# An mLSTM mixer kernel: moving one weight residual behind xd, summing blocks 2 and 3 first, and doubling x's last columns on ScalarE in the last batch

## The chip, the cores and the metric

The kernel runs on one core of a Trainium2 chip. The metric is the device time of one execution in microseconds (us), as the median over several runs. The engines are named as in the profile: PE is TensorE (PEld its weight loads), DVE is VectorE, ACT is ScalarE, POOL is GpSimd, and SP issues the DMAs.

## The reference

Two parts follow each other. An mLSTM attention runs over 4 batches, 8 heads, 768 steps and head size 40; its output is x, 768 x 320 in each batch. Then a mixer works on x:

```
h  = np.maximum(x.T @ w_tok1, 0) @ w_tok2      # over tokens, 768 -> 256 -> 768
u  = x + h.T
h2 = np.maximum(u @ w_ch1, 0) @ w_ch2          # over channels, 320 -> 1536 -> 320
out = u + h2
```

## The kernel before

The recurrence is computed in chunks of 128 steps, so each batch has six blocks of 128 tokens, numbered s = 0 to 5. Matrix products keep float32 accuracy by splitting each operand into a high part and a low residual (names that end in h and l) and summing three products. The attention of batch b+1 is issued in small steps between the mixer's matmuls of batch b.

In the mixer of one batch, `a_part` (L698) and `a_end` (L706) make the first token product. `phase_b` (L734) then makes the second token product of block s in a PSUM bank ps_b. It adds the product to x on VectorE (`add_x`, L737) and calls `split_x` (L741), which makes xd: the last 64 columns of x twice side by side. In batches 1 to 3 xd is one VectorE copy (L745). In batch 0 its first half is a ScalarE copy (L747), and its second half is a subtraction on GpSimd (L748). `phase_t` (L751) transposes block s on PE with three matmuls (L760 to L762, the third one reads xd). ScalarE copies the high part into uT (L763), and VectorE writes the low parts (L764, and L766 in batches 1 to 3).

The channel products follow in slots. Batches 0 and 3 are "wide": in each of the first 12 slots, `gemm1w` (L793) multiplies one 128-column piece of c1 by blocks 0 to 3 at once (512 columns, L800). `gemm2w` (L807) adds the results of the slot before into four accumulators: blocks 0 and 1 in the banks ps_acc (k = 0), blocks 2 and 3 in ps_m (k = 1). When the last piece (i = 11) is in, `end` (L820) adds each sum to x on VectorE (L823) and sends the block out. Blocks 4 and 5 go through narrower slots after that (`gemm1`, L772, and `gemm2`, L826).

Every engine takes its instructions in the order in which the Python code emits them. In the last batch this order is written out by hand: the full `phase_b` of blocks 0 and 1, and then

```
for s in range(4):
    phase_t(b, s, ss)
    phase_b(b, s + 2)
```

In batch 0 the order around the change is: blocks 0 and 1 through `phase_b`, `dec_hi` (ScalarE rounds two weight pieces to their high parts, L682), `dec_low` (GpSimd makes both low residuals, L688), blocks 2 and 3 through `phase_b`, then the transposes. `dec_low` takes all the residuals that wait in the list `lows`.

In batch 0, slot 12 is the first slot after the wide ones. It runs `gemm1` of block pair 2, then both halves of `gemm2w` for i = 11, and then six steps of the next batch's attention, which take the next ps_m bank for the output po (L432, L438).

Of the kernel before, what the change touches and what calls it, by code (L numbers as in the profile page):

```python
# [12 lines left out]
AF = mybir.ActivationFunctionType  # L13
# [4 lines left out]
B, H, S, D = 4, 8, 768, 40  # L18
# [16 lines left out]
def kernel(ctx: ExitStack, tc: tile.TileContext, gates, qk, q3, kv, og,  # L35
                            wt1, wt2, wc1, wc2, ident, out):
    nc = tc.nc
# [9 lines left out]
    def f32(x):  # L47
        return x.bitcast(F32)
# [578 lines left out]
    his, lows, wx, early = [], [], [], [True]  # L627
# [54 lines left out]
            nc.scalar.activation(d[0][:, a:a + WP], f, AF.Copy)  # L682
            lows.append((f, d, a))

    def dec_low():
        while lows:
            f, d, a = lows.pop(0)
            nc.gpsimd.tensor_tensor(d[1][:, a:a + WP], f, f32(d[0][:, a:a + WP]), ALU.subtract)  # L688


    def mm3(ps, pairs, first, last):
        n = len(pairs)
        for i, (a, m) in enumerate(pairs):
            nc.tensor.matmul(ps, a, m, start=(first and i == 0), stop=(last and i == n - 1))  # L694
# [39 lines left out]
    def phase_b(b, s, pool=(ps_m, "m"), add=True):  # L734
        return [*halves_b(b, s, pool, add)][-1]
# [5 lines left out]
    def split_x(b, s):  # L741
        x = xs[(b, s)][0]
        xd = lp.tile([128, 2, 64], F32R, tag="xd", name="xd", bufs=3)
        if b:
            nc.vector.tensor_copy(f32(xd), x[:, 256:320].unsqueeze(1).to_broadcast([128, 2, 64]))  # L745
        else:
            nc.scalar.activation(xd[:, 0], x[:, 256:320], AF.Copy)  # L747
            nc.gpsimd.tensor_tensor(xd[:, 1], x[:, 256:320], f32(xd[:, 0]), ALU.subtract)  # L748
        XD[(b, s)] = f32(xd)

    def phase_t(b, s, pool=(ps_m, "m")):  # L751
        x = xs[(b, s)][0]
        k = s // 2
        xd = XD.pop((b, s))
        if s == 0:
            UP[b] = lp.tile([128, 2, 5, 256], F32R, tag="uT", name="uT", bufs=1)
        u = U[(b, k)] = UP[b][:, k % 2]
        a = slice((s % 2) * 128, (s % 2) * 128 + 128)
        ps = pool[0].tile([128, 3, 128], F32, tag=pool[1], name="ps_t")
        nc.tensor.transpose(ps[:, 0, :], x[:, 0:128], id_t)  # L760
        nc.tensor.transpose(ps[:, 1, :], x[:, 128:256], id_t)
        nc.tensor.transpose(ps[:, 2, :], xd.rearrange("p a c -> p (a c)"), id_t)  # L762
        nc.scalar.activation(u[:, 0:3, a], ps, AF.Copy)  # L763
        nc.vector.tensor_tensor(u[:, 3:5, a], ps[:, 0:2, :], f32(u[:, 0:2, a]), ALU.subtract)  # L764
        if b:
            nc.vector.tensor_tensor(u[64:128, 2, a], ps[64:128, 2, :], f32(u[64:128, 2, a]), ALU.subtract)  # L766
# [23 lines left out]
    def wide(b):  # L790
        return b in (0, B - 1)
# [15 lines left out]
    def gemm2w(b, i, gh, gl, half=None):  # L807
        if i == 0 and half != 1:
            for k, (pool, tag) in enumerate(((ps_acc, "acc"), (ps_m, "m"))):
                acc[k] = [pool.tile([128, DM], F32, tag=tag, name=f"acc{j}") for j in range(2)]  # L810
        a = slice(i * DM, (i + 1) * DM)
        tiles = [(k, tt, slice(tt * 128, (tt + 1) * 128)) for k in range(2) if half in (None, k) for tt in range(2)]
        for k, tt, t in tiles:
            mm3(acc[k][tt], [(gh[:, k, t], c2[x][:, a]) for x in range(2)], i == 0, False)
        for k, tt, t in tiles:
            mm3(acc[k][tt], [(gl[:, k, t], c2[0][:, a])], False, i == NF - 1)
            if i == NF - 1:
                end(b, k, tt)

    def end(b, k, tt):  # L820
        s = 2 * k + tt
        x = xs[(b, s)][0]
        nc.vector.tensor_tensor(x, acc[k][tt], x, ALU.add)  # L823
        nc.sync.dma_start(out=out[b, s * 128:(s + 1) * 128, :], in_=x)
# [15 lines left out]
    def step(g, n=1):  # L840
        for _ in range(n):
            next(g, None)
# [150 lines left out]
    for b in range(B):  # L993
        if b:
            for j in range(2):
                for s in range(NC - 1):
                    a_part(b, j, s)
        if b == 1:
            step(ag)
        if b:  # L1000
            gemm2(*pend, half=0)
        for j in range(2):
            a_part(b, j, NC - 1)
            a_end(b, j)
        if b:
            gemm2(*pend, half=1)
            pend = None
            first = [halves_b(b, s) for s in range(2)]
            for g in first * 2 if b < B - 1 else first:
                step(g, 1 if b < B - 1 else 2)  # L1010
            if b < B - 1:
                phase_b(b, 2, ss)
                phase_t(b, 0)
                phase_t(b, 1)
                step(ag, 2)
                phase_b(b, 3, ss)
            else:
# [3 lines that stand above are left out]
                step(ag)  # L1021
        slots = [(k, p) for k in range(3) for p in range(6)]
        if b == 0:
            pf = prep_first(units[NC], units[NC + 1])
            cols()
            sp.release()
            wx += [tc.alloc_tile_pool(name="wx", bufs=1, side="right"), nxt[0]]
            ep.release()
            pp.release()
            lp = ctx.enter_context(tc.tile_pool(name="lp", bufs=2))  # L1030
            step(dg, 9)
            dec_load(nxt[2] + 7)
            dg = dec_ops(9)
            phase_b(b, 0)
            phase_b(b, 1)
            dec_hi()
            dec_low()
            step(dg, 1)
            phase_b(b, 2, ss)
            step(dg, 1)  # L1040
            phase_b(b, 3, ss)
            phase_t(b, 0)
            phase_t(b, 1)
            add_x(b, 4, phase_b(b, 4, ss, add=False))
            phase_t(b, 2)
            phase_t(b, 3)
            t5 = phase_b(b, 5, ss, add=False)
            step(dg, 9)
            add_x(b, 5, t5)
            dec_hi()  # L1050
        more = {1: [(phase_b, 4, ss)], 2: [(phase_t, 2, ss), (phase_t, 3, ss)], 5: [(phase_b, 5, ss)],
                6: [(phase_t, 4), (phase_t, 5, ss)]}
        for n, (k, p) in enumerate(slots):
            if b == 0 and 2 < n < 11:
                step(dec_ops(9), 9)
            if wide(b) and n < NF:
                g = gemm1w(b, n, 1 if n < 1 else 0 if b else 2)
            else:
                g = gemm1(b, k, p, 1 if n == 0 else 0)
            if b == 0:  # L1060
                if n < 3:
                    dec_hi()
                    dec_abs(nxt[2] + 2, both=True)
                    dec_low()
                    step(dec_ops(9, order=((0, 0), (0, 1), (1, 0), (1, 1))), 9)
                if n == 2:
                    for _ in range(2):
                        dec_hi(1)
                        dec_abs(nxt[1] + 1)
                    dec_low()  # L1070
                if n == 10:
                    split_x(0, 4)
                    split_x(0, 5)
                if n == 11:
                    phase_t(0, 4, ss)
                    phase_t(0, 5, ss)
                    gemm2(*pend)
                    pend = None
                    wx[0].release()
                    wq.release()  # L1080
                    xpool[1] = ctx.enter_context(tc.tile_pool(name="xp", bufs=1, side="right"))
                    step(ag)
                if n < 11:
                    if n > 2:
                        dec_abs(nxt[2] + 2)
                        dec_hi()
                        dec_low()
                    if n in (8, 9):
                        sigmoid(1, (n - 8,))
                    if n > 5:  # L1090
                        step(pf)
                elif n > 11:
                    o = STEPS0[n - 12]
                    step(ag, o[0])
                    gemm2(*pend, half=0)
                    step(ag, o[1])
                    gemm2(*pend, half=1)
                    pend = None
                    step(ag, o[2])
            else:  # L1100
                for f, *a in more.get(n, ()) if not wide(b) else ((phase_t, 4, ss), (phase_t, 5, ss)) if n == 11 else ():
                    f(b, *a)
                step(ag, STEPS[n])
            if pend:
                gemm2(*pend)
            pend = (b, k, n if wide(b) and n < NF else p) + g
# [53 lines left out]
```

## Time and profile before

| | |
|---|---|
| median of 3 runs | 428.86 us (428.62 to 430.13) |
| the profiled execution | 428.82 us, of which the traced span is 426.9 us |
| granted TensorE clock over the span | 1.00 |
| busy: PE, PEld, DVE, ACT, POOL | 98%, 93%, 68%, 43%, 34% |

The busy share of PE comes from modelled ends of pipelined matmuls, so the distance between two starts tells more than the end of one. The times below are microseconds from the start of the span.

### The profile page before, as it was taken

How to read it: one execution, taken by the hardware profiler on the slowest of the kernel's cores; microseconds unless marked ns; L12 is line 12 of the kernel's file. 1: busy time of each engine (PE TensorE's matmuls, PEld its weight loads, DVE VectorE, ACT ScalarE, POOL GpSimd, SP SyncE). 2: the span in 40 equal slices, each digit the busy share in tenths (PEclk: the TensorE clock that was granted, in tenths of full speed). 3: DMA queues.
4: the chain of work that ended last, by engine and by line, in shares of the span. 5: the costliest groups of instructions: out<-in, count | busy, mean ns of one | idle time of the engine just before them, and what ended most of it. 6: DMA issues, size and time to landing. Idle time of an engine off the chain costs nothing.

```text
span 426.9 us, 9017 instructions
## 1 busy us (share of the span) xinstructions
PE 419.8 (98%) x3509; PEld 396.5 (93%) x3510; DVE 291.4 (68%) x650; ACT 185.1 (43%) x426; POOL 143.1 (34%) x186
## 2 busy tenths in 40 slices
PE   8999999999999999999999999999999999999996
PEld 4888988988999999999999999999999998888996
DVE  8989778735676688788796698789786647111412
ACT  5977567893544635234224246334144112111111
POOL 7587476852453411341341230331350110000000
PEclk9999999999999999999999999999999999999999
DMA  7997747860968612334455031432320000000000
GB/s 215 274 280 251 247 128 247 279 195 29 264 191 239 220 54 66 115 117 110 148 160 187 28 107 33 145 114 90 124 85 32 0 20 15 0 2 0 30 33 31
DMA packets 24574, 52.34 MB, mean 123 GB/s; under 512 B 2565, under 2 KB 13325, under 8 KB 24533
## 3 DMA queue, kind: packets, MB, share of 16 engines
q1 hardware_dynamic: 24293, 51.61, 39.7%
q8 instruction: 27, 0.44, 0.4%
q10 hardware_dynamic: 240, 0.18, 0.2%
q14 instruction: 14, 0.11, 0.1%
HBM read 47.73 MB, written 4.04 MB: 121 GB/s over the span
## 4 chain that ended last, share of the span: by engine, by line
PE 90%; DMA 4%; DVE 2%; POOL 2%; ACT 1%; issue 1%; SPq 0%; POOLq 0%; ACTq 0%
PE acc L694 30%; PE ps_h L781 21%; PE ps_h L800 10%; PE ps_a L694 5%; PE ps_sc L312 5%; PE ps_b L694 4%; PE po L438 4%; PE po L408 3%; PE pu L385 2%; DMA wst<-in_wt_dram 2%; PE po L414 2%; DMA kvt<-in_kv_dram 1%; PE po L377 1%; PE ps_t L760 1%; PE ps_t L762 1%
## 5 line engine op out<-in xcount | busy, mean ns | idle before, releaser
L781 PE MATMUL ps_h<-uT,c1h 128*128 128x256 f32 x480 | 93.4, 282 | 0.0
L694 PE MATMUL acc<-c2h,gh 128*128 128x320 f32 x288 | 89.3, 319 | 0.0
L786 ACT ACTIVATE gh<-ps_h 128x512 fp32r<-128x512 f32 x48 | 28.6, 596 | 135.5 <-PE ps_h L781 135.5
L694 PE MATMUL acc<-c2l,gh 128*128 128x320 f32 x288 | 86.4, 309 | 0.0
L781 PEld LDWEIGHTS ps_h<-uT,c1h 128*128 128x128 f32 x480 | 76.9, 188 | 0.5
L781 PE MATMUL ps_h<-uT,c1l 128*128 128x256 f32 x288 | 74.3, 280 | 0.0
L787 DVE SCALAR_TENSOR_TENSOR gl<-ps_h,gh 128x512 fp32r<-128x512 f32 x48 | 33.0, 688 | 43.8 <-ACT gh L786 43.8
L694 PE MATMUL acc<-c2h,gl 128*128 128x320 f32 x288 | 61.9, 309 | 0.0
L694 PEld LDWEIGHTS acc<-c2h,gh 128*128 128x128 f32 x288 | 54.1, 188 | 1.6
L694 PEld LDWEIGHTS acc<-c2l,gh 128*128 128x128 f32 x288 | 54.2, 188 | 0.9
L781 PEld LDWEIGHTS ps_h<-uT,c1l 128*128 128x128 f32 x288 | 54.3, 188 | 0.0
L457 POOL TENSOR_TENSOR sig<-sig,ht 128x320 f32<-128x320 f32 x18 | 14.8, 820 | 99.4 <-DVE ht L418 91.2
L293 ACT ACTIVATE dd<-dd,bcol 128x128 f32<-128x128 f32 x144 | 45.8, 392 | 4.6 <-POOL dd L283 4.5
L694 PEld LDWEIGHTS acc<-c2h,gl 128*128 128x128 f32 x288 | 47.2, 188 | 0.1
L804 DVE SCALAR_TENSOR_TENSOR gl<-ps_h,gh 128x512 fp32r<-128x512 f32 x24 | 16.5, 689 | 41.1 <-ACT gh L803 41.1
L800 PE MATMUL ps_h<-uT,c1h 128*128 128x512 f32 x120 | 36.0, 394 | 0.0
L508 POOL TENSOR_TENSOR xl<-x,xh 128x320 fp32r<-128x320 f32 x18 | 15.8, 875 | 51.1 <-DVE xh L506 49.7
L322 DVE TENSOR_TENSOR dd<-ps_sc,dd 128x512 f32<-128x512 f32 x48 | 30.9, 681 | 2.6 <-PE ps_sc L312 2.6
L803 ACT ACTIVATE gh<-ps_h 128x512 fp32r<-128x512 f32 x24 | 14.2, 592 | 36.3 <-PE ps_h L800 36.3
L312 PE MATMUL ps_sc<-raw 64*128 64x128 f32 (+1 forms) x384 | 27.0, 282 | 0.0
L312 PEld LDWEIGHTS ps_sc<-raw 64*128 64x128 f32 (+1 forms) x384 | 23.2, 187 | 3.6 <-issue 1.8
L800 PEld LDWEIGHTS ps_h<-uT,c1h 128*128 128x128 f32 x120 | 22.1, 188 | 3.9
(153 smaller groups left out, 870.3 us busy)
## 6 DMA issues: line engine op xcount, KB each, us to landing
dd<-phi_d SPq DMA_DIRECT2D x18, 512.0 KB
wst<-in_wc_dram SPq DMA_DIRECT2D x22, 384.0 KB
kvt<-in_kv_dram SPq DMA_DIRECT2D x24, 324.0 KB
raw<-in_qk_dram SPq DMA_DIRECT2D x48, 160.0 KB
sig<-in_og_dram SPq DMA_DIRECT2D x8, 480.0 KB
out_dram<-x SPq DMA_DIRECT2D x24, 160.0 KB
q3t<-in_q_dram SPq DMA_DIRECT2D x20, 180.0 KB
wst<-in_wt_dram SPq DMA_DIRECT2D x8, 384.0 KB
```

Of the source, the lines that this page charges most:

```text
L293: nc.scalar.activation(dd[:, h, :], dd[:, h, :], AF.Exp, bias=bcol[:, c, HP * b + h:HP * b + h + 1])
L312: nc.tensor.matmul(t["s"][hf][:, h, :], r[:, 1, h, :], r[:, 0, h, :], start=True, stop=True)
L322: nc.vector.tensor_tensor(dd, t["s"][hf], dd, ALU.mult)
L438: nc.tensor.matmul(o, t["dd"][:, ROW[h], :], x, start=c == 0 and h == 0, stop=h == H - 1)
L457: nc.gpsimd.tensor_tensor(sg, sg, ht[:, :, 0:D], ALU.mult)
L508: nc.gpsimd.tensor_tensor(xl, x, f32(xh), ALU.subtract)
L694: nc.tensor.matmul(ps, a, m, start=(first and i == 0), stop=(last and i == n - 1))
L781: nc.tensor.matmul(ps[:, j, :], c1[x][:, a:a + 128], u[:, y, :], start=part is first and i == 0 and (order == 0 or j == 0), stop=i == len( ...
L786: nc.scalar.activation(gh, ps, AF.Relu)
L787: nc.vector.scalar_tensor_tensor(gl, ps, 0.0, f32(gh), op0=ALU.max, op1=ALU.subtract)
L800: nc.tensor.matmul(ps, c1[x][:, a:a + 128], u[:, :, y, :], start=n == 0, stop=n == len(todo) - 1)
L804: nc.vector.scalar_tensor_tensor(gl, ps, 0.0, f32(gh), op0=ALU.max, op1=ALU.subtract)
```

## The change

In batch 0 one of the two waiting residuals stays where it was, and the other goes behind the xd of blocks 2 and 3 on GpSimd. The other calls of `dec_low` take up to four, which is all that waits there. In the wide slots, blocks 2 and 3 are summed ahead of blocks 0 and 1; where the sum is split in halves, the first half is now blocks 2 and 3. In the last batch xd is made by one ScalarE instruction of 128 columns.

```diff
-    def dec_low():
-        while lows:
+    def dec_low(n=4):
+        for _ in range(min(n, len(lows))):
...
         if b:
-            nc.vector.tensor_copy(f32(xd), x[:, 256:320].unsqueeze(1).to_broadcast([128, 2, 64]))
+            last2 = x[:, 256:320].unsqueeze(1).to_broadcast([128, 2, 64])
+            if b < B - 1:
+                nc.vector.tensor_copy(f32(xd), last2)
+            else:
+                nc.scalar.activation(f32(xd), last2, AF.Copy)
...
-        tiles = [(k, tt, slice(tt * 128, (tt + 1) * 128)) for k in range(2) if half in (None, k) for tt in range(2)]
+        tiles = [(k, tt, slice(tt * 128, (tt + 1) * 128)) for k in (1, 0) if half in (None, 1 - k) for tt in range(2)]
...
             phase_b(b, 0)
             phase_b(b, 1)
             dec_hi()
-            dec_low()
+            dec_low(1)
             step(dg, 1)
             phase_b(b, 2, ss)
             step(dg, 1)
             phase_b(b, 3, ss)
+            dec_low()
             phase_t(b, 0)
```

## Rows read from the trace of the kernel before

**Rows 1.** The page, chain that ended last: share of the span by engine.
```profile
PE 90%; DMA 4%; DVE 2%; POOL 2%; ACT 1%; issue 1%; SPq 0%; POOLq 0%; ACTq 0%
```

**Rows 2.** Busy time by stretch: each engine, granted clock, DMA share, GB/s.
```profile
343.00:362.00 19.00, 18.98 (x123) 17.91 (x122) 11.15 (x30) 4.03 (x8) 1.51 (x2) 1.00 0.05 19
362.00:398.00 36.00, 36.00 (x203) 32.36 (x201) 6.89 (x10) 5.83 (x10) 0.00 (x0) 1.00 0.00 0
```

**Rows 3.** Waits of PE's weight loads: who waited for whom, total, times, longest.
```profile
PEld po L438 <- DVE x L823: 0.4, 1, 0.4
```

**Rows 4.** Timeline of POOL, batch 0: start, us, engine line operation.
```profile
53.53 1.98 POOL L688 TENSOR_TENSOR c1l<-wf,c1h 128x384 fp32r<-128x384 f32 x2
55.47 0.60 POOL L748 TENSOR_TENSOR xd<-x,xd 128x64 fp32r<-128x64 f32 x2
```

**Rows 5.** Timeline of PE, batch 0: transposes of blocks 2 and 3, and slot 1.
```profile
56.02 0.27 PE L762 MATMUL ps_t<-id_t,xd 128*128 128x128 f32 x1
...
56.41 0.27 PE L762 MATMUL ps_t<-id_t,xd 128*128 128x128 f32 x1
...
60.44 0.86 PE L800 MATMUL ps_h<-uT,c1l 128*128 128x512 f32 x3
```

**Rows 6.** Timeline of PE behind slot 12, and the same pair of products later.
```profile
104.80 0.73 PE L385 MATMUL pu<-kvt,kw 128*120 128x123 f32 x6
105.81 1.98 PE L438 MATMUL po<-kvt,dd 128*128 128x41 f32 x16 [0.29 <-DVE x L823]
...
120.32 0.77 PE L385 MATMUL pu<-kvt,kw 128*120 128x123 f32 x6
120.92 1.92 PE L438 MATMUL po<-kvt,dd 128*128 128x41 f32 x16
```

**Rows 7.** Timeline of DVE behind slot 12.
```profile
104.48 1.68 DVE L823 TENSOR_TENSOR x<-acc,x 128x320 f32<-128x320 f32 x4
```

**Rows 8.** Timeline of DVE, last batch.
```profile
352.13 0.23 DVE L745 COPY xd<-x 128x128 f32<-128x128 f32 x1
352.49 0.49 DVE L739 TENSOR_TENSOR x<-ps_b,x 128x320 f32<-128x320 f32 x1
...
353.34 0.42 DVE L764 TENSOR_TENSOR uT<-ps_t,uT 128x256 fp32r<-128x256 f32 x1
...
354.10 0.49 DVE L739 TENSOR_TENSOR x<-ps_b,x 128x320 f32<-128x320 f32 x1
...
354.77 0.42 DVE L764 TENSOR_TENSOR uT<-ps_t,uT 128x256 fp32r<-128x256 f32 x1
```

**Rows 9.** Timeline of ACT, last batch: first and last of four.
```profile
352.81 0.49 ACT L763 ACTIVATE uT<-ps_t 128x384 fp32r<-128x384 f32 x1 [2.53 <-PE ps_t L762]
...
356.72 0.49 ACT L763 ACTIVATE uT<-ps_t 128x384 fp32r<-128x384 f32 x1 [0.93 <-PE ps_t L762]
```

**Rows 10.** Timelines of PEld and PE, last batch: block 3's transpose and slot 0.
```profile
356.13 0.14 PEld L760 LDWEIGHTS ps_t<-id_t,x 128*128 128x128 f32 x1 [0.25 <-issue]
...
357.41 0.40 PE L800 MATMUL ps_h<-uT,c1h 128*128 128x512 f32 x1
```

**Rows 11.** ACT's groups by form: count, busy us, mean ns of one.
```profile
L489 ACT ACTIVATE xh<-x 128x320 fp32r<-128x320 f32 x6 | 2.8, 463 | 1.7 <-DVE x L484 1.7
...
L747 ACT ACTIVATE xd<-x 128x64 fp32r<-128x64 f32 x6 | 1.4, 250 | 2.1 <-DVE x L739 1.6 <-PE ps_t L761 0.6
```

**Rows 12.** Timelines of ACT and DVE, batch 0: xd behind the additions.
```profile
52.04 0.26 ACT L747 ACTIVATE xd<-x 128x64 fp32r<-128x64 f32 x1 [1.07 <-DVE x L739]
...
54.60 0.26 ACT L747 ACTIVATE xd<-x 128x64 fp32r<-128x64 f32 x1 [0.59 <-PE ps_t L761]
54.77 0.85 ACT L763 ACTIVATE uT<-ps_t 128x384 fp32r<-128x384 f32 x2
...
51.38 0.49 DVE L739 TENSOR_TENSOR x<-ps_b,x 128x320 f32<-128x320 f32 x1
...
54.02 0.49 DVE L739 TENSOR_TENSOR x<-ps_b,x 128x320 f32<-128x320 f32 x1
```

## The prediction

> **What bounds the kernel now.** I read the chain that ended last first: PE holds 90% of it [rows 1], so only what moves a start on PE moves the time. Then I read busy time by stretch, for the places that the diff touches. In the last batch PE is busy for 18.98 of 19.00 us while the token product and the transposes run, and for 36.00 of 36.00 us in the wide slots behind them. [...] So a loss ahead of the last batch's slots has no slack to go into: it reaches the end whole. The same holds for a gain. Then I took PE's waits. The one that has to do with the change is 0.4 us behind an addition of L823 [rows 3]. Last came the timelines of each engine around the three edits, from which all durations below are taken.
>
> **Edit 1, the residual on GpSimd (batch 0): 0.** GpSimd made both residuals from 53.53 on in 1.98 us (0.99 each), then the xd of blocks 2 and 3 in 0.60 us, done at 56.07 [rows 4]. With one residual behind them, xd of block 2 is done about 1 us earlier, and that of block 3 waits for its first half on ScalarE (54.60 + 0.26 = 54.86 [rows 12]) and is done near 55.3. But PE read them only at 56.02 and 56.41 [rows 5], 0.25 and 0.34 us after each was there (55.77 and 56.07): it was not waiting for them. The gain is between 0 and 0.1 us (the hop from GpSimd to PE, if it is longer than I think); I take 0. The moved residual is ready near 55.3 + 0.99 = 56.3 instead of 55.51. It belongs to slot 1, where PE first reads that low part at 60.44 [rows 5], so 4 us cover the delay. GpSimd's sum of work is unchanged, and what queues behind it there starts about 0.2 us later.
>
> **Edit 2, blocks 2 and 3 first: a gain of 0.40 us.** It counts where i = 11 ends in batch 0. VectorE adds the four sums from 104.48 on in 1.68 us, 0.42 each [rows 7]. The next attention needs the ps_m bank of block 2, which is third in line: PE's po starts at 105.81, 1.01 us after pu at 104.80. Where nothing is missing, the same two stand 0.60 us apart (120.32 and 120.92) [rows 6]. With block 2 first its bank is free 0.8 us earlier, so po starts at 104.80 + 0.60 = 105.40: a gain of 0.41, the wait's own row says 0.4 [rows 3]. I take 0.40, with bounds 0 (the next step is late for another reason) and 0.41. Late next are the attention's own operands, and what they wait for on ScalarE, VectorE and GpSimd starts from po and moves with it. Blocks 0 and 1 now leave ps_acc last. That is when block 2 left before: 0.42 x 4 behind 104.48, still 106.16. The next user comes one slot later. The four output DMAs change places on SP's queue, but the last of them is issued when it was. In the last batch the same order changes no start, since the adds follow each other in the same way and the first narrow sum comes a slot later.
>
> **Edit 3, xd on ScalarE (last batch): a loss of 2.7 us.** This removes six VectorE copies of 0.23 us [rows 8] and adds six ScalarE instructions. What matters is ScalarE's order. The loop emits the transpose of s, then `phase_b` of s + 2. So ScalarE's queue becomes xd0, xd1, uT0, xd2, uT1, xd3, uT2, xd4, uT3, xd5. Before, uT1 needed only PE's transposes. Now it stands behind xd2, which waits for block 2's addition on VectorE, which stands behind uT0's low parts there. Each block now passes through one closed loop over VectorE and ScalarE:
> - from the start of the first low part (L764) to the addition: 354.10 - 353.34 = 0.76 [rows 8];
> - the addition: 0.49 [rows 8];
> - hop to ScalarE: block 3's addition in batch 0 ends at 54.02 + 0.49 = 54.51 and xd starts at 54.60, so 0.09; in block 0 it was 52.04 - 51.87 = 0.17 [rows 12];
> - from the start of xd to the start of uT: 0.17 for 64 columns [rows 12]. A column costs (463 - 250) / 256 = 0.83 ns [rows 11], so 64 more columns add 0.05: 0.22;
> - uT: 0.49, and the hop to VectorE 353.34 - 353.30 = 0.04 [rows 8, 9].
>
> The sum is 2.09 us for a block. Before, the low parts of two blocks stood 354.77 - 353.34 = 1.43 apart [rows 8]. The first turn starts from block 1's addition, which ends at 352.49 + 0.49 = 352.98. Then xd1 starts at 353.07 and uT0 at 353.29, where it was 352.81. Three loops later uT3 starts at 353.29 + 3 x 2.09 = 359.56 (it was 356.72 [rows 9]) and ends at 360.05. The first matmul of slot 0 reads all four blocks and so needs uT3. It starts near 360.09 (with the same hop of 0.04) and not at 357.41 [rows 10], 2.68 us later. PE has nothing else to do there: the token products of blocks 4 and 5 are ahead of it in its queue and end earlier. Its small wait of 0.25 us at block 3 [rows 10] lies inside this time.
>
> The bounds: the least hop in the rows is 0.04 and the least distance 0.17, which makes a loop of 1.99 us and a loss of 2.28. The longest hop of 0.17 with xd at its full length (250 + 64 x 0.83 = 303 ns, no overlap) makes 2.25 us and a loss of 3.32. I take the middle values, since their rows are the same lines of this kernel.
>
> The rows show an overlap on ScalarE: uT starts 0.17 us behind the start of an xd that lasts 0.26 [rows 12]. [...]
>
> **The sum.** 0 - 0.40 + 2.68 = 2.28 us. The profiled execution took 428.82, its span 426.9 with 1.9 around it, 0.04 under the median of 428.86. From the median the sum gives 431.14, rounded 431.1. With the bounds of edits 2 and 3: 428.86 - 0.41 + 2.28 = 430.7 to 428.86 + 3.32 = 432.2.
>
> **The rivals.**
> - *VectorE is relieved, and nothing is held up: 428.3 (not slower).* This decides at one place: whether uT1 stands behind xd2 in ScalarE's queue. If uT1 went first, VectorE would be 0.23 us shorter in each block, PE's wait of 0.25 at block 3 [rows 10] would shrink to about nothing, and with the 0.40 of edit 2 the time would be 428.86 - 0.2 - 0.40. For it speaks that the copies do sit on the engine that PE waits for there. Against it: in batch 0 ScalarE ran xd of block 3 at 54.60 and only then the first uT [rows 12], in the order of the code. I give it 0.10.
> - *TensorE's clock falls in the new wait: 432.5 to 434.9.* PE would stand for about 1.5 us ahead of slot 0, the longest wait since the start. All stretches here have the upper clock [rows 2], and there is no row at the lower level to price it from. If the 16 matmuls of slots 0 and 1, which stand (0.86 - 0.40) / 2 = 0.23 us apart [rows 5, 10], took up to twice as long, it would cost up to 3.7 us more than the forecast. [...] The price goes by the rows, and for the chance I count that shorter waits before left the clock alone: 0.05.
> - *Only the first and last turns cost, as the additions come earlier than I think: 429.5 to 430.2.* If uT0 were not held behind xd1, 0.48 us would go, which gives 430.2 at the lower bounds. A loop without one hop and one overlap more would give less. I give 0.05.
>
> **How the numbers follow.** The forecast has 0.80. Its own range is 430.7 to 432.2, and to hold 8 times in 10 the range reaches down to the 430.2 of the last rival and up to 432.4 for the start of the clock's case. About 0.5%, here 2.14 us or 431.0, is what a measurement of this kernel tells from no change. The forecast lies just above it. With the bounds at +1.9 and +3.3 I put 0.62 of its chance above the line: 0.50 slower and 0.30 same. The clock adds 0.05 to slower; the relief and the short loop add 0.15 to same, less 0.02 for a relief that goes further than I see, and a few hundredths stay open among these: slower 0.55, same 0.43, faster 0.02.
>
> **What would show it.** In the changed profile, ACT's timeline in the last batch should alternate xd and uT with starts of uT near 353.3, 355.4, 357.5 and 359.6 (less 0.4 for edit 2). Each xd should begin right behind an addition, and PE should idle about 1.5 us ahead of the first L800 with ACT's uT as the releaser. PE's wait for L823 near 105 should be gone. GpSimd's xd of blocks 2 and 3 should end near 54.9 and 55.3, with PE's transposes where they were. The prediction is wrong if uT's starts stay 1.2 to 1.4 us apart, if slot 0 starts before 359, or if the granted clock falls below 1.00 there.

## The result, and the profile after

The changed kernel took 431.70 us (median of 6 runs) against 428.83 for the kernel before in the same comparison: a ratio of 1.0065, with a 95% interval of 1.0045 to 1.0084. That is slower by 2.9 us. The forecast was 431.1 in a range of 430.2 to 432.4, so the prediction held. The profiled execution took 431.58 us, and its span is 429.6.

The page of the changed kernel, busy time and the chain that ended last:

```profile
PE 420.3 (98%) x3509; PEld 396.6 (92%) x3510; DVE 292.8 (68%) x644; ACT 186.4 (43%) x432; POOL 143.0 (33%) x186
...
PE 86%; DVE 9%; issue 1%; POOL 1%; ACT 1%; DMA 1%; POOLq 0%; DVEq 0%; ACTq 0%
```

PE did the same work (3509 matmuls), but it holds 86% of the chain and not 90% [rows 1]. VectorE stands in it with 9%, although six copies left that engine. Most of the 9% has nothing to do with the change: 18.6 us of it lie in the first 40 us of the span and 12.6 us between 250 and 340 us, and three later profiles of the same kernel have 5%, 2% and 5%. But 4.1 us lie in the last batch, where the chain ran over PE alone before. Now it goes round over VectorE and ScalarE there (the chain in the changed kernel in order of time: start, us, engine, tile, line):

```profile
354.67 0.50 DVE x L739
...
355.20 0.31 ACT xd L749
355.51 0.39 ACT uT L767
...
355.92 0.42 DVE uT L768
...
356.36 0.29 DVE uT L770
```

What this costs PE is shown by busy time in stretches of the changed kernel (columns as in [rows 2]):

```profile
343.00:362.00 19.00, 17.01 (x110) 15.68 (x109) 9.47 (x23) 4.25 (x12) 1.67 (x2) 1.00 0.05 18
...
362.00:398.00 36.00, 36.00 (x200) 32.36 (x200) 7.59 (x11) 6.57 (x11) 0.00 (x0) 1.00 0.00 1
```

PE is busy for 17.01 of 19.00 us ahead of the wide slots, where it was busy for 18.98 [rows 2]. Behind that it is full, as before. The clock is 1.00 in both. The reason is in ScalarE's timeline of the last batch in the changed kernel (L749 is xd, L767 is uT):

```profile
353.19 0.31 ACT L749 ACTIVATE xd<-x 128x128 f32<-128x128 f32 x1 [0.57 <-DVE x L739]
353.41 0.47 ACT L767 ACTIVATE uT<-ps_t 128x384 fp32r<-128x384 f32 x1
355.20 0.31 ACT L749 ACTIVATE xd<-x 128x128 f32<-128x128 f32 x1 [1.32 <-DVE x L739]
355.42 0.47 ACT L767 ACTIVATE uT<-ps_t 128x384 fp32r<-128x384 f32 x1
357.27 0.31 ACT L749 ACTIVATE xd<-x 128x128 f32<-128x128 f32 x1 [1.38 <-DVE x L739]
357.48 0.47 ACT L767 ACTIVATE uT<-ps_t 128x384 fp32r<-128x384 f32 x1
359.34 0.31 ACT L749 ACTIVATE xd<-x 128x128 f32<-128x128 f32 x1 [1.38 <-DVE x L739]
359.55 0.47 ACT L767 ACTIVATE uT<-ps_t 128x384 fp32r<-128x384 f32 x1
```

The reader is to see two things. Before, each uT waited for PE's transpose alone [rows 9]. Now none does: each follows its xd by 0.21 to 0.22 us. And ScalarE stands idle ahead of each xd until VectorE's addition is done, for 0.57 us at the first one shown and for 1.3 to 1.4 us at the others. VectorE's timeline of the same kernel is the other half of the loop:

```profile
353.91 0.42 DVE L768 TENSOR_TENSOR uT<-ps_t,uT 128x256 fp32r<-128x256 f32 x1 [0.76 <-ACT uT L767]
...
354.67 0.49 DVE L739 TENSOR_TENSOR x<-ps_b,x 128x320 f32<-128x320 f32 x1
355.92 0.42 DVE L768 TENSOR_TENSOR uT<-ps_t,uT 128x256 fp32r<-128x256 f32 x1 [0.75 <-ACT uT L767]
...
356.68 0.49 DVE L739 TENSOR_TENSOR x<-ps_b,x 128x320 f32<-128x320 f32 x1
```

VectorE waits for uT and then makes the addition that the next xd waits for. Its low parts stand 355.92 - 353.91 = 2.01 us apart, where they stood 1.43 apart [rows 8]. PE pays at block 2, at block 3 and ahead of slot 0 (PE's timeline, changed kernel; the first row is the stage's first token product):

```profile
350.70 0.31 PE L694 MATMUL ps_b<-rh,w2h 128*128 128x320 f32 x1
...
355.31 0.30 PE L764 MATMUL ps_t<-id_t,x 128*128 128x128 f32 x1 [0.21 <-DVE x L739]
...
357.32 0.30 PE L764 MATMUL ps_t<-id_t,x 128*128 128x128 f32 x1 [0.54 <-DVE x L739]
...
360.08 0.50 PE L804 MATMUL ps_h<-uT,c1h 128*128 128x512 f32 x1 [1.23 <-ACT uT L767]
```

From the first token product to slot 0 it takes 360.08 - 350.70 = 9.38 us. Before, it was 357.41 [rows 10] less 350.53, the same matmul's start in the kernel before: 6.88.

```profile
350.53 0.31 PE L694 MATMUL ps_b<-rh,w2h 128*128 128x320 f32 x1
```

This distance, called the stage below, is the measure for all experiments, since it repeats from one execution to the next: it is 9.37 or 9.38 us in all four traces of the changed kernel, whose spans lie between 429.3 and 430.4 us.

The other edits, in PE's timeline of the changed kernel:

```profile
55.78 0.27 PE L766 MATMUL ps_t<-id_t,xd 128*128 128x128 f32 x1
...
56.17 0.27 PE L766 MATMUL ps_t<-id_t,xd 128*128 128x128 f32 x1
...
104.55 0.73 PE L385 MATMUL pu<-kvt,kw 128*120 128x123 f32 x6
105.12 1.91 PE L438 MATMUL po<-kvt,dd 128*128 128x41 f32 x16
```

Behind slot 12, po follows pu by 0.57 us and not by 1.01 [rows 6]: the wait is gone. In this trace the gain does not last to the last batch, though: from pu to the stage's first token product it takes 246.15 us (104.55 to 350.70), and it took 245.73 before (104.80 to 350.53). The transposes of xd stand 0.39 us apart as before (56.02 and 56.41 in [rows 5]), though GpSimd had their xd ready at 55.02 (54.26 + 0.76) and not at 56.07 [rows 4], in the changed kernel:

```profile
53.29 1.01 POOL L688 TENSOR_TENSOR c1l<-wf,c1h 128x384 fp32r<-128x384 f32 x1
54.26 0.76 POOL L752 TENSOR_TENSOR xd<-x,xd 128x64 fp32r<-128x64 f32 x2
54.98 1.00 POOL L688 TENSOR_TENSOR c1l<-wf,c1h 128x384 fp32r<-128x384 f32 x1
```

### The profile page after: what moved, and what is told of

It reads as the page before. It is cut to its first block, busy times and chain, and to the rows that moved or that the text cites. A ratio compares the mean times of both kernels' runs of the same rounds, so it can differ in the third digit from the quotient of the medians.

```text
span 429.6 us, 9017 instructions
## 1 busy us (share of the span) xinstructions
PE 420.3 (98%) x3509; PEld 396.6 (92%) x3510; DVE 292.8 (68%) x644; ACT 186.4 (43%) x432; POOL 143.0 (33%) x186
## 4 chain that ended last, share of the span: by engine, by line
PE 86%; DVE 9%; issue 1%; POOL 1%; ACT 1%; DMA 1%; POOLq 0%; DVEq 0%; ACTq 0%
PE acc L694 29%; PE ps_h L785 20%; PE ps_h L804 10%; PE ps_a L694 5%; PE ps_sc L312 5%; PE po L438 4%; PE ps_b L694 3%; PE po L408 3%; PE pu L385 3%; PE po L414 2%; PE po L377 1%; DVE dd L322 1%; DVE x L739 1%; DMA q3t<-in_q_dram 1%; DVE uT L768 1%
```

## The experiments

**Theory:** ScalarE takes its instructions in order, so the uT of block s stands behind the xd of block s + 1, and a loop over VectorE and ScalarE paces the stage. **Rivals:** ScalarE's copy and the hop to another engine cost time wherever they stand; the other two edits have part in the loss; the clock falls.

The kernel before was timed anew with each set of runs: 428.84 us beside the first four, 429.39 beside the next four, 429.43 beside the last three.

**xd back on VectorE.**

```diff
-            if b < B - 1:
-                nc.vector.tensor_copy(f32(xd), last2)
-            else:
-                nc.scalar.activation(f32(xd), last2, AF.Copy)
+            nc.vector.tensor_copy(f32(xd), last2)
```

> The changed kernel with xd of the last batch back on VectorE (the other two edits stay). Theory (ScalarE's uT of block s stands behind xd of block s + 1, so each block passes through a closed loop of about 2.07 us): uT's starts in the last batch go back to 1.2 to 1.4 us apart, slot 0's first matmul stands 6.9 us behind the first token product of the stage (350.53 to 357.41 before, 350.70 to 360.08 after), and the time is 428.86 - 0.4 = 428.4 us, or up to 428.9 if the gain at slot 12 is given back later as the changed trace suggests. Rival (the other two edits cost part of the 2.9 us): over 429.5.

Measured: 428.54 us, ratio 0.9995 (0.9985 to 1.0004); stage 6.87 us. The loss is gone with this one edit, and the other two together do no harm that can be measured.

**The ScalarE xd alone.** The kernel before, with only the lines above put in.

> The kernel before with the ScalarE xd of the last batch alone. Theory (this edit is the whole loss): 2.6 us over the kernel before, 431.4 to 431.7, with uT's starts 2.0 to 2.1 us apart and slot 0 about 9.4 us behind the stage's first token product. Rival (it takes the three edits together, or some of the loss is elsewhere): under 430.5.

Measured: 432.76 us, ratio 1.0095 (1.0075 to 1.0114); stage 9.38 us. The stage is what the theory asks for to the hundredth, but the time is 1 us above the expectation. Two of the six executions have a mean granted clock of 0.996 and the longest spans (431.0 and 431.5); the other four have 1.00 and spans of 429.2 to 430.7. In three of the six, 2.9 to 3.2 us lie outside the span. This opened the question of the clock again, which the last two parts of this section take up.

**Same instructions, other order.** The six ScalarE xd stay. Each is emitted behind the uT of the block before it; ahead of the loop only xd of block 0 is made (those lines are left out here).

```diff
...
                 for s in range(4):
                     phase_t(b, s, ss)
-                    phase_b(b, s + 2)
+                    split_x(b, s + 1)
+                    add_x(b, s + 2, phase_b(b, s + 2, add=False))
+                split_x(b, NC - 1)
```

> The changed kernel with the six ScalarE xd of the last batch kept, but emitted in another place: xd of block s + 1 behind uT of block s, not ahead of it. Same instructions on the same engines, only ScalarE's order differs. Theory (the order holds uT up, not ScalarE's length or the hop): uT's starts are 1.2 to 1.3 us apart again, slot 0 is 6.6 to 7.0 us behind the stage's first token product, and the time is 428.1 to 428.6. Rival (ScalarE's slower copy and the hop to another engine cost the time wherever they stand): still over 430.5, with uT's starts near 2 us apart.

Measured: 428.81 us, ratio 0.9999 (0.9984 to 1.0014), the median slightly above the expected 428.1 to 428.6; stage 6.85 us. ScalarE's timeline in this kernel:

```profile
351.99 0.49 ACT L767 ACTIVATE uT<-ps_t 128x384 fp32r<-128x384 f32 x1 [0.42 <-PE ps_t L766]
352.38 0.30 ACT L749 ACTIVATE xd<-x 128x128 f32<-128x128 f32 x1
353.21 0.49 ACT L767 ACTIVATE uT<-ps_t 128x384 fp32r<-128x384 f32 x1 [0.53 <-PE ps_t L766]
353.80 0.31 ACT L749 ACTIVATE xd<-x 128x128 f32<-128x128 f32 x1
354.54 0.49 ACT L767 ACTIVATE uT<-ps_t 128x384 fp32r<-128x384 f32 x1 [0.42 <-PE ps_t L766]
```

The same copies last as long (0.31 us), and uT waits for PE again, 1.2 to 1.3 us apart. This run decides: 2.5 us of the stage (9.38 less 6.85) hang on the place of the copies in ScalarE's queue. In the new place their length and the hop cost nothing that can be measured (6.85 beside the 6.88 of the kernel before).

**xd on GpSimd.**

```diff
-                nc.scalar.activation(f32(xd), last2, AF.Copy)
+                nc.gpsimd.tensor_copy(f32(xd), last2)
```

> The changed kernel with xd of the last batch on GpSimd, which has nothing else to do there. Theory (only what stands in ScalarE's queue ahead of uT costs): no closed loop, since GpSimd holds nobody up; PE may wait for xd at the third transpose by 0.1 to 0.4 us in a block, and VectorE loses its six copies: 428.2 to 429.2. Rival (taking xd off the engine that makes x costs a hop in each block, on any engine): 430.5 to 431.5.

Measured: 428.24 us, ratio 0.9995 (0.9983 to 1.0006); stage 6.80 us, the shortest of all. The copies go to another engine here too and start 0.06 to 0.07 us behind the end of the addition (in the loop on ScalarE it was 0.04 to 0.10), but nothing that PE or VectorE waits for queues behind them. GpSimd's group of these copies, by form:

```profile
L749 POOL COPY xd<-x 128x128 f32<-128x128 f32 x6 | 1.8, 293 | 11.2 <-DVE x L739 11.2
```

It has the lowest median of the runs, but the interval does not set it apart from the kernel before.

**Only the first two xd on ScalarE.**

```diff
-            if b < B - 1:
+            if b < B - 1 or s > 1:
```

> The changed kernel with only the first two xd of the last batch (blocks 0 and 1) on ScalarE, the other four back on VectorE. Theory (closed loop): only the first turn is left. uT of block 0 still stands behind xd of block 1 and starts 0.4 to 0.5 us later than before within its stage, but no later uT waits behind an xd: slot 0 stands 7.2 to 7.4 us behind the stage's first token product (before 6.88, changed 9.38), and the time is 428.7 to 429.1. Rival (each xd on ScalarE costs its share of the 2.5 us): two of six give 0.8 us, slot 0 at 7.7 us and 429.3.

Measured: 429.28 us, ratio 0.9999 (0.9983 to 1.0014); stage 7.27 us, not the 7.7 of the rival. The timeline of ScalarE in this kernel shows one late turn, and then uT waits for PE again:

```profile
353.09 0.31 ACT L749 ACTIVATE xd<-x 128x128 f32<-128x128 f32 x1 [0.57 <-DVE x L739]
353.31 0.47 ACT L767 ACTIVATE uT<-ps_t 128x384 fp32r<-128x384 f32 x1
354.15 0.49 ACT L767 ACTIVATE uT<-ps_t 128x384 fp32r<-128x384 f32 x1 [0.37 <-PE ps_t L766]
```

The 0.39 us over the stage before are about the first turn's delay: uT of block 0 starts 2.70 us behind the stage's first token product (350.61 to 353.31), and 2.28 before (350.53 to 352.81 [rows 9]). The clocked times do not resolve a loss of this size: the ratio is 1, and whether edit 2's gain, which is in this kernel too, makes up for it is not shown. The time itself lies above the expected 429.1, as the kernel before does on that occasion.

**The order of sums alone.** The kernel before with the new `tiles` line of `gemm2w`.

> The kernel before with the new order of sums alone (blocks 2 and 3 first). Theory: po behind slot 12 follows pu by 0.57 to 0.6 us and not by 1.0, VectorE's addition of block 2 is first, and the time is 0.3 to 0.45 us less, 428.4 to 428.6, which five rounds may not tell from no change. Rival (the gain is eaten by later waits on VectorE): 428.8, with the 0.4 us gone again by 350 us of the span.

Measured: 428.57 us, ratio 0.9994 (0.9975 to 1.0012). The interval does not tell it from no change. In its trace po follows pu by 0.57 us (105.78 and 106.35). But the gain is gone again by the last batch there, as the rival has it: from pu to the stage's first token product it takes 246.38 us, with a new wait of PE of 0.87 near 145 us, where it took 245.73 before. Five other kernels' traces with the new order have 245.1 to 245.3, and keep it. So the order takes away the wait behind slot 12 every time, and whether the gain arrives varies from execution to execution.

**Each xd twice on ScalarE.**

```diff
-                nc.scalar.activation(f32(xd), last2, AF.Copy)
+                for _ in range(2):
+                    nc.scalar.activation(f32(xd), last2, AF.Copy)
```

> The changed kernel with each ScalarE xd of the last batch issued twice (the second writes the same values again). Theory: the second copy holds ScalarE for another 0.22 us in each of the four turns ahead of uT, so uT's starts are 2.25 to 2.35 us apart, slot 0 stands 9.38 + 4 x 0.22 = 10.2 to 10.4 us behind the stage's first token product, and the time is 0.8 to 1.0 us over the changed kernel. Rival (the turn is set by the hops between the engines, and ScalarE's length hides in them): no more than 0.2 us over the changed kernel.

Measured: 433.05 us, ratio 1.0096 (1.0066 to 1.0126), beside 432.50 for the changed kernel on the same chip; stage 10.62 us. ScalarE's timeline in this kernel:

```profile
355.14 0.65 ACT L750 ACTIVATE xd<-x 128x128 f32<-128x128 f32 x2 [1.32 <-DVE x L739]
355.70 0.47 ACT L768 ACTIVATE uT<-ps_t 128x384 fp32r<-128x384 f32 x1
357.49 0.65 ACT L750 ACTIVATE xd<-x 128x128 f32<-128x128 f32 x2 [1.32 <-DVE x L739]
358.05 0.47 ACT L768 ACTIVATE uT<-ps_t 128x384 fp32r<-128x384 f32 x1
```

The stage grows by 1.24 us, 0.31 a turn, and not by the expected 0.22: two xd last 0.65 together, so the second starts 0.34 behind the first, while a uT starts 0.22 behind an xd. The time rose by less than the stage and less than expected (0.55 us), with four runs here against six. The rival falls: ScalarE's occupied time counts in each turn.

**The changed kernel, three times more.**

> The changed kernel once more, for a second profile and more times. Theory: the last batch repeats itself (uT's starts 2.0 to 2.1 us apart, slot 0 9.3 to 9.5 us behind the stage's first token product), while the small waits between 106 and 350 us of the span fall out differently, so that the time lies between 430.8 and 431.8. Rival (the small waits on VectorE near 143 and 293 us belong to the change): they are there again at the same places with 0.2 to 0.3 us each.

> The changed kernel, a third profile. Theory: the stage to slot 0 is 9.38 us again and the clock 1.00 in most executions. Rival (the waits of 0.2 to 1.5 us are enough for the clock to fall in some executions): a stretch at the lower clock behind slot 0's wait in this or the next profile, with a span 1 to 4 us longer.

> The changed kernel, a fourth profile, for the same question as the third: the stage to slot 0 is 9.38 us, and either the clock stays at 1.00 in all stretches, or a stretch behind slot 0's wait shows the lower level.

Measured: 432.50, 432.33 and 431.81 us, with ratios of 1.0091 (1.0057 to 1.0126), 1.0071 (1.0044 to 1.0099) and 1.0051 (1.0024 to 1.0078). All three times are at or above the 431.8 that I had expected as the upper end of the first. The stage is 9.37, 9.38 and 9.38 us, and the clock is 1.00 in all three traces. Of the small waits, the one of PE on VectorE near 293 us is in two of these three traces and in the first one, but not in the third profile, and a kernel with the same instructions up to 350 us (xd on VectorE) does not have it either. The one near 143 us is in one of these three, and the ScalarE xd alone has it too. Both come and go in one and the same program. In all the traces with the wait near 293 us, one VectorE xd shortly ahead of it lasts about 1.1 us in place of 0.23 (the first profile of the changed kernel):

```profile
285.58 1.10 DVE L747 COPY xd<-x 128x128 f32<-128x128 f32 x1
```

The lower clock did occur in executions that left no trace. Of 27 executions of the changed kernel, seven have a mean clock of 0.992 to 0.996. None of 66 of the kernel before and none of 56 of the kernels with a short stage is below 0.998.

**Each xd four times on ScalarE,** `range(4)` in the edit above.

> The changed kernel with each ScalarE xd of the last batch issued four times with the same values, to make PE's waits there longer and see what the clock does. Theory of the loop alone: each further copy holds ScalarE for 0.31 to 0.34 us in each of the four turns, so the stage to slot 0 is 9.38 + 3 x 4 x 0.32 = 13.1 to 13.5 us, the span about 4 us over the changed kernel, and the granted clock stays 1.00. Rival (the clock gives way when PE waits long enough, as the mean clock of 0.992 to 0.996 in five of the 22 longer runs hints): a stretch behind the waits with a granted clock near 0.5, in which the 512-column matmuls stand further apart than 0.23 us, and a span 1 us or more longer still.

Measured: 437.10 us, ratio 1.0177 (1.0100 to 1.0254), of two runs; stage 13.70 us, above the expected 13.1 to 13.5, since the copies of block 0 hold up the xd of block 1 by another 0.35 us. In this trace the clock falls (busy time by stretch: PE, PEld, DVE, ACT, POOL, granted clock, DMA share, GB/s):

```profile
354.00:358.00 4.00, 2.62 (x18) 2.10 (x17) 1.21 (x3) 2.52 (x9) 0.00 (x0) 1.00 0.00 0
358.00:362.00 4.00, 2.56 (x16) 2.09 (x16) 1.77 (x5) 1.97 (x6) 0.00 (x0) 1.00 0.00 0
362.00:366.00 4.00, 1.80 (x6) 1.25 (x6) 1.86 (x5) 1.85 (x6) 0.00 (x0) 0.59 0.00 0
366.00:370.00 4.00, 4.00 (x12) 3.15 (x11) 0.69 (x1) 1.60 (x5) 0.00 (x0) 0.56 0.00 0
370.00:374.00 4.00, 4.00 (x24) 3.55 (x23) 0.69 (x1) 0.60 (x1) 0.00 (x0) 1.00 0.02 4
...
363.00:369.00 6.00, 4.52 (x11) 3.56 (x12) 1.29 (x4) 3.16 (x10) 0.00 (x0) 0.50 0.00 0
```

The stretches with 0.59 and 0.56 hold both levels, as the last row shows: from 363 to 369 us it is the lower one throughout. Ahead of it PE waited 0.85 to 0.87 us for xd three times, 0.54 and 0.55 for two additions, and 2.20 ahead of slot 0.

PE's timeline of the same kernel, two matmuls of slot 0 and two of slot 2:

```profile
365.50 0.63 PE L805 MATMUL ps_h<-uT,c1h 128*128 128x512 f32 x1
365.92 0.63 PE L805 MATMUL ps_h<-uT,c1l 128*128 128x512 f32 x1
...
372.58 0.39 PE L805 MATMUL ps_h<-uT,c1l 128*128 128x512 f32 x1
372.81 0.39 PE L805 MATMUL ps_h<-uT,c1h 128*128 128x512 f32 x1
```

The matmuls stand 0.42 us apart where the granted clock is 0.50 and 0.23 where it is 1.00, and from slot 0 to the end of the span it takes 71.8 us (436.3 - 364.48) in place of 69.5 (426.9 - 357.41): the fall costs 2.3 us here. The theory that the clock stays falls. What its rival says is seen here in one trace, behind these longer waits. That the seven executions of the changed kernel have the same cause, in the same place, is likely, since only kernels with the long stage show it, but none of them left a trace.

## Why the prediction was right, step by step

- **Edit 3, the loop: right, and 0.18 us too long.** Forecast 2.68 us, shown 9.38 - 6.88 = 2.50. A turn was put at 2.09 and measured 2.01, 2.07 and 2.07. The hop from the addition to xd, put at 0.09, was 0.04 twice and 0.10 twice; the distance from xd to uT, put at 0.22, was 0.21 to 0.22; uT lasted 0.47, not 0.49. The start of slot 0 then costs 0.11 us more that I did not count: its second matmul follows the first by 0.34 us instead of 0.23 (360.08 and 360.42; before 357.41 and 357.64). The wait did not fall on PE in one piece: 1.23 us stand ahead of slot 0, where about 1.5 was forecast, and 0.21 and 0.54 at blocks 2 and 3. The loss reaches the end whole, as forecast: from slot 0's second matmul to the end of the span it takes 69.2 us, and 69.3 before.
- **The overlap on ScalarE held.** xd lasts 0.31 us, near the 303 ns worked out from the rows. But the uT behind it starts after 0.21 to 0.22: the distance is shorter than the copy.
- **Edit 2: right behind slot 12, not shown at the end.** Forecast 0.40 us, shown 1.01 - 0.57 = 0.44 in the changed trace. That a gain reaches the end whole was not borne out there: it is gone by 350 us, and in the eleven traces with the new order the time from pu to the last batch's stage varies from 245.12 to 246.38 us, by more than the gain. Alone it is too small for the clocked times to resolve.
- **Edit 1: right as far as the traces go.** GpSimd had the two xd ready by 55.0, and PE's transposes kept their distance. It was not run alone, but three kernels of the record are without it. In all thirteen traces the first transpose of block 2 stands 1.93 to 1.94 us behind that of block 0, and slot 12's pu 49.0 us behind that, with the edit and without it: it gives and costs nothing up to there.
- **"VectorE is relieved" was wrong, at the place that I named for it:** uT does stand behind xd. The run with the other order shows what that rival would have given: a stage of 6.85 us, 0.03 shorter than before and not the 0.2 that I had counted. The rival in which only the first and last turns cost fell too: three full turns follow the first.
- **The clock was not all or nothing.** I gave it 0.05 and a price of up to 3.7 us for every execution. The factor of up to two in that price was an estimate that no row showed; the run with four copies has 0.42 us against 0.23, a factor of 1.8, at a granted clock of 0.50. In the changed kernel a lower clock appears in 7 of 27, and those have a median span of 431.3 us where the other 20 have 429.6, so 1.7 us. This lifts the later medians, but not the 431.7: all six executions behind it have a clock of 0.999 or 1.00. In the executions at a clock of 0.998 and more, the span rose from 427.25 (before, 66 executions) to 429.6, by 2.35 us, beside the forecast of 2.28.
- **What stays open:** why 431.7 lies 0.6 us above 431.1. Nearly all of it is time outside the span, which was 2.7 to 2.8 us in three of the first six executions of the changed kernel and 1.7 to 2.0 in the others, a median of 2.35 where the 66 of the kernel before have 1.76. Values of 2.6 to 3.0 occur in 9 of those 66 as well, and no trace shows what lies there. If it is chance how many of them fall among six executions, so is this distance from the forecast.

## What to carry to other kernels

Before an instruction is moved to an idle engine, write down that engine's queue with the new instruction in it, and ask what stands behind it and what it waits for: an early uT became late because an xd of the next block, which was not yet possible, stood ahead of it. The busy share of ScalarE (43%) said nothing about that. The same six copies cost 2.5 us of the stage in one place of the queue (9.38 us) and nothing one place later (6.85), or on an engine whose queue nobody waits for (6.80).

## What the runs showed of the hardware that was not expected

The waits of PE in the last batch of the changed kernel (0.21, 0.54 and 1.23 us) go with a lower mean clock (0.992 to 0.996) in 7 of 27 executions of one and the same program, and none of the 122 executions of kernels without the full loop is below 0.998. And the time from a 128-column copy on ScalarE to the next instruction differed with what followed it in these traces: 0.21 to 0.22 us to a uT, and 0.34 us (0.65 for two, less the 0.31 of one) to a second copy that writes the same place. Where each xd is issued four times, the last copy of one xd is followed at once by the first copy of the next (two instructions, 0.51 us together):

```profile
353.41 0.51 ACT L750 ACTIVATE xd<-x 128x128 f32<-128x128 f32 x2
```

The second of them is a copy of x's last columns like the repeated ones, but by the same reckoning (0.51 less 0.31) it starts about 0.2 us behind the first. So 0.34 us do not stand between any two such copies: here they were measured between copies with the same source and the same place, and which of the two decides was not tried.
